# Attention and a bilinear feed-forward on one core: float64 weight words loaded two bytes off, their upper half made by a float16 conversion, raw words and gate outputs in planned slots

## The chip, the cores and the metric

The kernel runs on one core of one Trainium2 chip. The metric is the device time of one execution in microseconds; three executions give a median. A trace of one more execution shows every instruction of the five engines: TensorE (PE, with its weight loads as PEld), VectorE (DVE), ScalarE (ACT), GpSimd (POOL) and SyncE (SP, which here only issues DMAs).

## What is computed

Random-feature attention over 8 batches, 8 heads, 576 positions and head size 64, and then a feed-forward with a product of two projections in the middle. The four weights of the feed-forward are float64 arrays (a division of a float32 draw by a square root makes them so); the other inputs are float32.

```python
def phi(x):                                  # x scaled by D ** -0.25
    h = x @ omega.T - (x * x).sum(-1, keepdims=True) / 2
    return np.exp(h - h.max(-1, keepdims=True)) / np.sqrt(m)
q_p, k_p = phi(q_s), phi(k_s)                # 128 features
kv, z = k_p.T @ v, k_p.sum(2)                # per batch and head
x = (q_p @ kv) / (q_p @ z + 1e-6)            # to (4608, 512)
out = ((x @ w1) * (x @ w2) @ w3) @ w_out     # w1, w2: 512 x 1024; w3: 1024 x 1024; w_out: 1024 x 512
```

## The kernel before

**Stages.** The 4608 positions are 36 chunks of 128 rows. Each chunk of k and of q goes through `features`: a projection on omega into a bank pair of PSUM (`pa`), its row maximum (DVE), an exponential (ACT), and a split of the result into a float16 part and its float16 remainder. Products are then made of three float16 matmuls (`PASSES`). `kv_batch` sums keys with values, `q_attend` divides, `x_turn` scales a chunk and has it transposed by a DMA into `xT`. `gate` multiplies two chunks at a time by w1 and w2, multiplies both results, and splits the product into `h`; `project_out` multiplies `h` by W and writes the output. From chunk 28 to 33 `pair_first` and `pair_rest` do the last product with fewer multiplications, on mixed blocks of W made by `mix`.

**Weights.** W is the product of w3 and w_out, made on the chip in `W_block` in float32: eight blocks, four for the first half of the inner sum and four for the second, which `keep` adds up in `Wb`. w1 and w2 are split into float16 pairs in place, in `w12b`, after their absolute sums have given a scale. All weights come as raw 64-bit words, 20 loads of 1 MB (the first in two halves), and go through `from_float64`: `fetch` issues the load, `magnitude` takes on ACT the absolute value of the upper words read as float32, and `words` clamps it (on GpSimd, but for the first half), shifts it, merges in sign and exponent bits, and finally merges in the shifted lower word. The last three are passes of DVE over 1024 numbers in each of 128 partitions.

**Places.** Raw words, magnitudes and the gate's outputs live in one tile, `arena`, of 21 blocks of 2 KB a partition: three raw places of four blocks, two of magnitudes, five free. `block` hands places out, `used` takes them back, in the order in which the program is written; after the last weights the raw places go to the free list. Converted w_out and w3 are guests in `w12b[:, 1]`, the place of the second halves of w1 and w2; those can be loaded only after the products are done, and the second half of w_out after the first four blocks.

**Order.** Nothing runs as it is written. A planner (`Plan`) records every operation with its tiles and dependencies. `forward` plays the program with a cost for every operation, takes on each engine the ready one of least rank, gives tiles of a pool their slots, and `order` ranks again from the end backwards. Each engine then gets its own fixed order, SP too. Where the plan leaves TensorE idle for longer than 516 ns, `fill` puts matmuls of a tile of ones on themselves (`ones_bf`, 128x512) whose result nothing reads; they keep TensorE active. They are called fillers here. As one function fires all operations, all lines of the profile are L171; instructions are told apart by tile and shape.

**Softmax.** `DQ` and `DK` give for each chunk how the maximum is subtracted: "0" is a DVE subtraction from PSUM into `e` and one exponential of 1024 numbers, "1" is eight exponentials of 128 numbers straight from PSUM with the negated maximum as bias. `DQ` has "1" for three of the 36 chunks of q.

Of the kernel before, what the change touches and what calls it, by code (L numbers as in the profile page):

```python
# [12 lines left out]
U32 = mybir.dt.uint32  # L13
AF = mybir.ActivationFunctionType
# [12 lines left out]
F64_LEAST, F64_TOP = 2.0**-15, float.fromhex("0x1.dffffep+16")  # L27
# [7 lines left out]
CLAMP = "dp"  # L35
# [4 lines left out]
DQ = '100110000000000000000000000000000000000000'  # L40
# [52 lines left out]
ARENA = 21  # L93
# [155 lines left out]
class Plan:  # L249
# [112 lines left out]

    def forward(self, rank, deps, after, costs, slots=False, backwards=False, scale=0.0):

        start, end, waiting, ready = {}, {}, {}, {n: [] for n in LANES}
        clock = dict.fromkeys(LANES, 0.0)
        est = {}
# [28 lines left out]
        for _ in self.ops:  # L396
# [26 lines left out]
            clock[n] = t + busy  # L423
            if op.method.startswith("dma"):
# [38 lines left out]
    def order(self):  # L463

        ops = self.ops
        costs = {o: self.cost(o) for o in ops}

# [83 lines left out]
ROOM = {}  # L551
BANKS = ("pm", "pa")
# [5 lines left out]
WARM = True  # L558
HOP = 80
ROUNDS = 1  # L560
# [5 lines left out]
def tile_favor_attention_then_bilinear_ffn(  # L566
# [27 lines left out]
    DF = w1.shape[1] // 2  # L594
    NC = HD // P
    NF = DF // P
    DO = wo.shape[1] // 2
# [405 lines left out]

    arena = const.tile([P, ARENA, 512], F32, name="arena")
    raw_at = list(range(0, 4 * RAW64_BUFS, 4))
    mag_at = list(range(4 * RAW64_BUFS, 4 * RAW64_BUFS + 4, 2))
    free = list(range(4 * RAW64_BUFS + 4, ARENA))

    def block():
        assert free, "no block left"  # L1010
        return free.pop(0)

    left = {}
# [4 lines left out]
    def used(at):  # L1018

        left[at] -= 1  # L1020
        if not left[at]:
            free.append(at)

    def from_float64(new, src, name, cuts=1):
# [4 lines left out]
        def fetch():  # L1029
            at = st["at"] = raw_at.pop(0)  # L1030
            nfetch[0] += 1
            raw = arena[:, at : at + 4].bitcast(U32).rearrange("p b i -> p (b i)")

            raw = raw.rearrange("p (j i) -> p j i", j=src.shape[1])
            step = src.shape[1] // cuts
            for k in range(0, src.shape[1], step):
                {'a': nc.scalar, 's': nc.sync, 'p': nc.gpsimd}[pick(FQ, nfetch[0])].dma_start(raw[:, k : k + step], src[:, k : k + step])
            st["raw"] = raw.rearrange("p j i -> p (j i)").rearrange("p (i t) -> p i t", t=2)

        def magnitude():  # L1040

            at = st["mag"] = mag_at.pop(0)
            st["g"] = arena[:, at : at + 2].rearrange("p b i -> p (b i)")
            st["dst"] = new()
            for a in pieces:
                nc.scalar.activation(st["g"][:, a], st["raw"][:, a, 1].bitcast(F32), AF.Abs)

        def words():
            for a in pieces:
                g, dst = st["g"][:, a], st["dst"][:, a].bitcast(U32)  # L1050
                top, low = st["raw"][:, a, 1], st["raw"][:, a, 0]

                (nc.gpsimd if pick(CLAMP, nfetched.pop(0)) == "p" else nc.vector).tensor_scalar(
                    g, g, F64_TOP, F64_LEAST, ALU.min, ALU.max
                )
                g = g.bitcast(U32)
                nc.vector.tensor_scalar(
                    g, g, 3, 0x3FFFFFFF, ALU.logical_shift_left, ALU.bitwise_and
                )
                nc.vector.scalar_tensor_tensor(  # L1060
                    g, top, 0xC0000000, g, ALU.bitwise_and, ALU.bitwise_or
                )
                last = nc.vector.scalar_tensor_tensor(
                    dst, low, 29, g, ALU.logical_shift_right, ALU.bitwise_or
                )
            return last

        def bits():
            converted.append(words())
            raw_at.append(st["at"])  # L1070
            mag_at.append(st["mag"])
# [6 lines left out]
    def w12_load(n, i):  # L1078
# [4 lines left out]
        src = w[cc * P : (cc + 2) * P, 1024 * i : 1024 * (i + 1)].rearrange("(c p) f -> p c f", p=P)  # L1083
# [30 lines left out]
    guest = w12b[:, 1]  # L1114

    def wo_load(n):
        j = 2 * n
        at = j % HALF
        dst = guest[:, at : at + 2].rearrange("p j o -> p (j o)")
        src = wo[j * P : (j + 2) * P].rearrange("(j p) o -> p j o", p=P)  # L1120
        return from_float64(lambda: dst, src, f"wo_{j}", cuts=1 if n or not START else 2)
# [3 lines left out]
    def W_block(n):  # L1125

        i, j0 = n * 2 % NF, n * 2 // NF * HALF
        at = HALF + n % 2 * 2
        w3c = guest[:, at : at + 2].rearrange("p b i -> p (b i)")
        pss = []  # L1130

        def product():
            w = w3c.rearrange("p (j i) -> p j i", j=HALF)
            for k in range(2):
# [3 lines left out]
                for j in range(HALF):  # L1138
# [3 lines left out]
                        guest[:, j],  # L1142
# [15 lines left out]
        src = w3T[j0 * P : (j0 + HALF) * P, 2 * i * P : 2 * (i + 2) * P]  # L1158
        return from_float64(lambda: w3c, src.rearrange("(j p) i -> p j i", p=P), f"w3_{n}") + [
# [27 lines left out]
    hs = {}  # L1187

    def gate(c0, n, u):
# [20 lines left out]
        if LATE <= c0 < LATE_END:  # L1210
# [10 lines left out]
            places = [block() for _ in range(2)]  # L1221
            hi, lo = (
                arena[:, k].bitcast(F16)[:, 0 : 7 * P].rearrange("p (m s) -> p m s", s=P)
                for k in places
# [3 lines left out]
            hs[c0, u] = (hi, lo), places  # L1228
# [351 lines left out]
```

## Time and profile before

| | |
|---|---|
| median of three executions | 799.29 us (798.73 to 800.18) |
| the profiled execution | 798.87 us |
| its span, first to last instruction | 797.1 us |
| busy: PE / DVE / ACT / POOL | 783.7 / 610.9 / 452.6 / 262.5 us |
| mean granted clock of TensorE | 0.997 of full speed |
| DMA | 88.42 MB, mean 111 GB/s |

Busy time is counted as the union of an engine's instructions. A row of a group has busy time in us and then the mean of one instruction in ns; instructions overlap at their ends, so that the mean times the count is more than the busy time. A row of the timeline begins with its start and its length in us, and a bracket at its end says how long the engine stood idle before it and what released it.

### The profile page before, as it was taken

What the parts mean: (1) busy time and instruction counts of PE and PEld (TensorE: products, weight loads), DVE (VectorE), ACT (ScalarE), POOL (GpSimd) and SP (SyncE); (2) the same over time, 40 slices, a digit from 0 to 9 for tenths busy, and PEclk for the clock granted to TensorE, in tenths of its full rate; (3) what the DMA queues carried; (4) which work ended last, traced back from release to release, by engine and by line L of the source; (5) the groups of instructions that cost most, each with busy time, mean ns of one, the idle gap of its engine ahead of it and who ended that gap; (6) DMA issues with size and microseconds to landing.
All of it is one profiled execution on the core that took longest, in us unless ns stands there. A gap on an engine that the chain in (4) does not pass through costs nothing.

```text
span 797.1 us, 20482 instructions
## 1 busy us (share of the span) xinstructions
PE 783.7 (98%) x8591; PEld 596.0 (75%) x8591; DVE 610.9 (77%) x1136; ACT 452.6 (57%) x807; POOL 262.5 (33%) x228
## 2 busy tenths in 40 slices
PE   8999999999899999999999999999999999999998
PEld 4554657978687777868787778777777777789886
DVE  6799999967986698598768767698879985996411
ACT  6885759866573566567545655476555535433211
POOL 2122212124443244234452443333343332333110
PEclk9999999999999999999999999999999999999999
DMA  9877875354361445455354444245543332223101
GB/s 333 301 230 252 226 184 117 67 108 95 93 132 42 108 119 107 73 128 120 80 95 133 87 87 95 73 114 112 106 77 54 81 81 55 54 54 67 42 1 53
DMA packets 142620, 88.42 MB, mean 111 GB/s; under 512 B 116736, under 2 KB 117120, under 8 KB 142528
## 3 DMA queue, kind: packets, MB, share of 16 engines
q1 hardware_dynamic: 142016, 86.07, 44.8%
q8 instruction: 67, 1.10, 0.6%
q10 hardware_dynamic: 432, 0.79, 0.3%
q0 software_dynamic: 80, 0.26, 0.1%
q14 instruction: 25, 0.20, 0.1%
HBM read 49.35 MB, written 9.44 MB: 74 GB/s over the span
## 4 chain that ended last, share of the span: by engine, by line
PE 75%; DVE 14%; ACT 6%; issue 3%; DMA 1%; SPq 0%; POOL 0%; DVEq 0%; ACTq 0%
PE pm L171 63%; PE pa L171 12%; DVE arena L171 3%; DVE s_nm L171 2%; DVE w12b L171 2%; DVE e L171 1%; ACT arena L171 1%; DVE ek L171 1%; ACT junk L171 1%; DVE vhl L171 1%; DMA arena<-w3T 1%; ACT vhl L171 1%; ACT ek L171 1%; DVE hl L171 1%; ACT e L171 1%
## 5 line engine op out<-in xcount | busy, mean ns | idle before, releaser
L171 PE MATMUL pm<-xT,w12b 128*128 128x256 f16 (+1 forms) x3840 | 392.7, 262 | 0.3 <-DMA xT<-xhl 0.3
L171 PEld LDWEIGHTS <-w12b 128*128 128x128 f16 x3840 | 338.9, 98 | 39.3 <-DMA xT<-xhl 1.3
L171 PE MATMUL pm<-Wb,arena 128*128 128x512 f16 (+1 forms) x852 | 173.2, 360 | 0.0
L171 PEld LDWEIGHTS <-arena 128*128 128x128 f16 x996 | 95.8, 98 | 79.4 <-issue 0.3
L171 POOL TENSOR_TENSOR arena<-asb,arena 128x512 f16<-128x512 f32 x60 | 80.5, 1341 | 158.4 <-ACT arena L171 145.4
L171 DVE TENSOR_REDUCE s_nm<-pa 128x8 f32<-128x1024 f32 x72 | 87.3, 1215 | 41.7 <-PE pa L171 41.7
L171 ACT ACTIVATE e<-e,ln_e,s_es 128x1024 f32<-128x1024 f32 x55 | 67.8, 1238 | 73.9 <-DVE e L171 73.7
L171 POOL TENSOR_TENSOR eq<-e,eq 128x1024 f16<-128x1024 f32 x31 | 74.0, 2387 | 95.3 <-issue 41.7
L171 POOL TENSOR_TENSOR ek<-e,ek 128x1024 f16<-128x1024 f32 x26 | 57.1, 2196 | 93.2 <-ACT ek L171 88.0
L171 DVE TENSOR_TENSOR e<-pa,s_nm 128x1024 f32<-128x1024 f32 x59 | 71.6, 1217 | 2.1 <-DVE s_nm L171 0.5
L171 DVE TENSOR_TENSOR asb<-pm,asb 128x512 f32<-128x512 f32 x60 | 41.1, 686 | 36.5 <-PE pm L171 35.6
L171 ACT CAST arena<-asb 128x512 f16<-128x512 f32 x60 | 36.8, 613 | 39.5 <-DVE asb L171 39.5
L171 PE MATMUL pm<-w12b 128*128 128x512 f32 x128 | 56.7, 596 | 0.3 <-DVE s_ws L171 0.3
L171 POOL TENSOR_SCALAR arena<-arena 128x1024 f32<-128x1024 f32 (+1 forms) x20 | 22.6, 1131 | 97.4 <-ACT arena L171 97.4
L171 ACT ACTIVATE asb<-pm 128x512 f32<-128x512 f32 x60 | 35.2, 586 | 32.8 <-PE pm L171 30.4
L171 PE MATMUL pa<-om,hl 64*128 64x128 f16 x1320 | 46.6, 218 | 3.2 <-DVE hl L171 3.2
L171 PEld LDWEIGHTS <-hl 64*128 64x128 f16 x1320 | 37.4, 95 | 14.7 <-issue 9.5
L171 DVE SCALAR_TENSOR_TENSOR xhl<-xs,s_p2r,xhl 128x512 f16<-128x512 f32 x36 | 38.9, 1080 | 12.0 <-ACT xhl L171 12.0
L171 ACT ACTIVATE o<-pm,oscs 128x512 f32<-128x512 f32 (+1 forms) x31 | 20.8, 671 | 47.9 <-PE pm L171 47.8
L171 PEld LDWEIGHTS pm<-w12b 128*128 128x128 f32 x128 | 23.8, 190 | 27.7 <-issue 26.3
L171 PE MATMUL pa<-vhl,ek 128*128 128x65 f16 (+1 forms) x896 | 43.3, 205 | 0.0
L171 DVE SCALAR_TENSOR_TENSOR hl<-qraw,s_s,hl 128x512 f16<-128x512 f32 x30 | 33.7, 1125 | 9.1 <-ACT hl L171 9.0
(116 smaller groups left out, 977.0 us busy)
## 6 DMA issues: line engine op xcount, KB each, us to landing
vraw<-v SPq DMA_DIRECT2D x36, 256.0 KB, 2.9
qraw<-qT SPq DMA_DIRECT2D x35, 256.0 KB, 2.8
arena<-w3T SPq DMA_DIRECT2D x8, 1024.0 KB, 5.9
kraw<-kT SPq DMA_DIRECT2D x32, 256.0 KB, 3.1
arena<-w SPq DMA_DIRECT2D x8, 1024.0 KB, 6.7
out<-o SPq DMA_DIRECT2D x28, 256.0 KB, 2.5
arena<-wo SPq DMA_DIRECT2D x3, 1024.0 KB, 4.9
out<-e SPq DMA_DIRECT2D x6, 256.0 KB, 2.1
```

The costliest lines, as they stand in the source:

```text
L171: p.real = getattr(lanes[p.lane], p.method)(*args, **{k: real(a) for k, a in p.kwargs.items()})
```

## The change

The load of raw words is issued in 16-bit units into a slot of 2050 words, one unit behind its start. So every 64-bit word lies two bytes off, and two of its parts fall on boundaries of their own: its top 16 bits are a bfloat16 number, and the 32 bits under them (bits 16 to 47) an aligned word. A copy on ACT from bfloat16 to float16 turns the top into sign, five exponent bits and the mantissa bits, which, with the lowest exponent bits that the bfloat16 mantissa carried along, are the upper half of the float32. It is written to every second 16-bit place of one of two constant tiles, `top`, whose other halves are zero. One DVE pass shifts the aligned word right by 13 and merges it with `top`. Absolute value, clamp, shift and merge of the sign are gone.

The arena goes. Raw words and gate outputs share four slots of one pool ("big", 8200 bytes a partition), converted w3 and w_out and the mixing's sums four of another ("mag", 4096 bytes), and the planner hands them out. A group's gate outputs (two chunks) are one slot. The converted w_out and w3 are no longer guests in `w12b`. All chunks of q take the eight exponentials. The planner runs two rounds in place of one, and counts the port that DVE and GpSimd share: `locks` names the operations that hold it. A smaller scratch for GpSimd's DMAs makes room.

```diff
-DQ = '100110000000000000000000000000000000000000'
+DQ = '1'
-ARENA = 21
+BIGS = 4
+MAGS = 4
+TOPS = 2
...
+    @staticmethod
+    def locks(op):
+
+        if op.lane == "gpsimd":
+            return not op.method.startswith("dma")
+        if op.lane != "vector" or op.out.space == PSUM or op.method in ("tensor_reduce", "reciprocal"):
+            return False
+        wide = [a for a in op.ins if a.free_size() > 1]
+        if op.out.free_size() == 1 or any(a.space == PSUM for a in wide):
+            return False
+        return True
...
-            t = est[op]
+            t = max(est[op], port) if LOCK and op.locks else est[op]
...
+            if op.locks:
+                port = t + busy
...
-ROUNDS = 1
+ROUNDS = 2
...
-            raw = arena[:, at : at + 4].bitcast(U32).rearrange("p b i -> p (b i)")
+            raw = at.tile([P, 2050], F32, tag="big", name=f"raw_{name}", bufs=BIGS)
+            st["top"] = tops[nfetch[0] % TOPS]
+            rows = raw.bitcast(U16)[:, 1:4097].rearrange("p (j i) -> p j i", j=src.shape[1])
...
+            st["hi"] = raw.bitcast(BF16)[:, 4:4100].rearrange("p (i t) -> p i t", t=4)[:, :, 0]
+            st["mid"] = raw.bitcast(U32)[:, 1:2049].rearrange("p (i t) -> p i t", t=2)[:, :, 0]
...
-                nc.scalar.activation(st["g"][:, a], st["raw"][:, a, 1].bitcast(F32), AF.Abs)
+                copy(kind == "d", to[:, a], st["hi"][:, a])
...
-                    g, g, F64_TOP, F64_LEAST, ALU.min, ALU.max
-                    g, g, 3, 0x3FFFFFFF, ALU.logical_shift_left, ALU.bitwise_and
-                    g, top, 0xC0000000, g, ALU.bitwise_and, ALU.bitwise_or
-                    dst, low, 29, g, ALU.logical_shift_right, ALU.bitwise_or
+                    dst[:, a], st["mid"][:, a], 13, top[:, a], ALU.logical_shift_right, ALU.bitwise_or
...
-    guest = w12b[:, 1]
+            g = at.tile([P, 1024], F32, tag="mag", name=f"wo_{j}", bufs=MAGS)
...
-        place = block()
+            parts[c0] = at.tile([P, 2 * n, 512], F32, tag="big", name=f"h_{c0}", bufs=BIGS)
...
-    nc = bacc.Bacc("TRN2", target_bir_lowering=False, num_devices=1)
+    nc = bacc.Bacc("TRN2", target_bir_lowering=False, num_devices=1, dynamic_dma_scratch_size=2048)
```

How instructions stand on DVE near the start of the program, from the first halves of w_out on. Before (`arena` holds raw words and magnitudes, `w12b` takes the converted ones, `s_nm` is a row maximum):

```order
L171 TENSOR_SCALAR arena<-arena 128x512
L171 TENSOR_SCALAR s_nm_214<-s_nm_214 128x8
L171 TENSOR_SCALAR pm_81<-pm_81 128x1
L171 SCALAR_TENSOR_TENSOR arena<-arena 128x512
L171 TENSOR_SCALAR arena<-arena 128x512
L171 SCALAR_TENSOR_TENSOR w12b<-arena 128x512
```

After (`big` holds raw words, `top` the upper halves, `mag` takes the converted ones):

```order
L173 SCALAR_TENSOR_TENSOR mag_82<-big_78,top_74 128x512
L173 TENSOR_SCALAR s_nm_231<-s_nm_231 128x8
L173 SCALAR_TENSOR_TENSOR mag_82<-big_78,top_74 128x512
L173 TENSOR_SCALAR pm_84<-pm_84 128x1 x2
L173 RECIPROCAL s_s_40_85<-pm_84 128x1
L173 TENSOR_SCALAR unom<-pm_84 128x1
L173 SCALAR_TENSOR_TENSOR mag_264<-big_147,top_75 128x1024
```

Each converted piece is now one instruction, and the second w_out load's stands ahead of the next row maximum.

On SP, which issues the loads in order, around the second half of w_out. Before (`w` is w1 or w2, `w3T` is w3, `wo` is w_out):

```order
L171 DMA vraw_86<-v 128x512
L171 DMA vraw_167<-v 128x512
L171 DMA vraw_169<-v 128x512
L171 DMA vraw_180<-v 128x512
L171 DMA arena<-w 128x2x1024
L171 DMA_TRANSPOSE eqT_101<-eq_100 128x8x128
L171 DMA arena<-w3T 128x4x512
L171 DMA_TRANSPOSE eqT_101<-eq_100 128x8x128
L171 DMA arena<-w 128x2x1024
L171 DMA arena<-wo 128x2x1024 x2
L171 DMA arena<-w3T 128x4x512 x2
```

After:

```order
L173 DMA big_147<-w 128x2x2048
L173 DMA big_159<-wo 128x2x2048
L173 DMA kraw_124<-kT 128x512
L173 DMA_TRANSPOSE eqT_104<-eq_103 128x8x128
L173 DMA big_172<-wo 128x2x2048
L173 DMA_TRANSPOSE eqT_104<-eq_103 128x8x128
L173 DMA big_78<-w3T 128x4x1024
L173 DMA vraw_89<-v 128x512
L173 DMA vraw_174<-v 128x512
L173 DMA vraw_185<-v 128x512
L173 DMA vraw_229<-v 128x512
```

The two w_out loads now stand apart, ahead of the loads of v for the next batch, which stood ahead of them.

## Rows read from the trace of the kernel before

**Rows 1.** Three stretches: span, busy us and instructions by engine, clock, DMA, GB/s.

```profile
0.00:40.00 40.00, 37.26 (x234) 21.16 (x234) 27.32 (x52) 29.43 (x76) 8.60 (x18) 1.00 0.89 317
40.00:160.00 120.00, 117.42 (x1133) 80.48 (x1132) 116.93 (x200) 90.69 (x175) 25.06 (x37) 1.00 0.67 179
160.00:797.10 637.10, 629.00 (x7231) 494.35 (x7228) 466.68 (x886) 332.46 (x558) 228.88 (x175) 1.00 0.39 85
```

**Rows 2.** Groups by shape, busy us and mean ns: the fillers.

```profile
L171 PE MATMUL pm<-ones_bf 128*128 128x512 bf16 x123 | 29.7, 393 | 1.1 <-DVE sums L171 1.1
```

**Rows 3.** Timeline of PE: first fillers, first weight product, last fillers, last product.

```profile
1.12 3.53 PE L171 MATMUL pm<-ones_bf 128*128 128x512 bf16 x9 [1.12 <-DVE sums L171]
...
24.57 7.05 PE L171 MATMUL pm<-w12b 128*128 128x512 f32 x16
...
129.68 1.48 PE L171 MATMUL pm<-ones_bf 128*128 128x512 bf16 x6
...
783.00 10.58 PE L171 MATMUL pm<-Wb,arena 128*128 128x512 f16 x72
```

**Rows 4.** Timeline of all engines, 16 to 25 us: one w3 conversion.

```profile
16.40 1.15 ACT L171 ACTIVATE arena<-arena 128x1024 f32<-128x1024 f32 x1
...
17.64 1.26 POOL L171 TENSOR_SCALAR arena<-arena 128x1024 f32<-128x1024 f32 x1 [2.33 <-ACT arena L171]
...
23.23 1.21 DVE L171 SCALAR_TENSOR_TENSOR w12b<-arena 128x1024 uint32<-128x1024 uint32 x1
```

**Rows 5.** Groups by shape: conversion, a plain ACT cast, a DVE split pass.

```profile
L171 DVE SCALAR_TENSOR_TENSOR arena<-arena 128x1024 uint32<-128x1024 uint32 x19 | 24.8, 1306 | 0.2
...
L171 DVE SCALAR_TENSOR_TENSOR w12b<-arena 128x1024 uint32<-128x1024 uint32 x19 | 24.1, 1276 | 0.1
...
L171 ACT ACTIVATE arena<-arena 128x1024 f32<-128x1024 f32 x19 | 22.1, 1163 | 6.1 <-DVE w12b L171 3.8 <-DMA arena<-w3T 1.3 <-DMA arena<-w 1.0
L171 POOL TENSOR_SCALAR arena<-arena 128x1024 f32<-128x1024 f32 x19 | 22.0, 1158 | 89.1 <-ACT arena L171 89.1
...
L171 DVE TENSOR_SCALAR arena<-arena 128x1024 uint32<-128x1024 uint32 x19 | 13.9, 734 | 5.4 <-POOL arena L171 5.3
...
L171 DVE SCALAR_TENSOR_TENSOR w12b<-w12b,s_ws 128x512 f16<-128x512 f32 x16 | 12.1, 759 | 0.7 <-ACT w12b L171 0.6
...
L171 ACT CAST eq<-e 128x1024 f16<-128x1024 f32 x6 | 6.3, 1054 | 0.1
```

**Rows 6.** Groups by shape: the two ways to the exponential.

```profile
L171 DVE TENSOR_TENSOR e<-pa,s_nm 128x1024 f32<-128x1024 f32 x59 | 71.6, 1217 | 2.1 <-DVE s_nm L171 0.5
L171 ACT ACTIVATE e<-e,ln_e,s_es 128x1024 f32<-128x1024 f32 x55 | 67.8, 1238 | 73.9 <-DVE e L171 73.7
...
L171 ACT ACTIVATE e<-pa,s_nm 128x128 f32<-128x128 f32 x48 | 13.5, 390 | 0.0
...
L171 DVE TENSOR_SCALAR s_nm<-s_nm 128x8 f32<-128x8 f32 x13 | 4.8, 369 | 0.0
```

**Rows 7.** Timeline of SP's issues: the first w_out loads, the late ones.

```profile
2.01 1.53 SPq L171 DMA_DIRECT2D arena<-wo  x3
...
51.85 6.52 SPq L171 DMA_DIRECT2D arena<-wo  x2
```

**Rows 8.** DMA issues: count, KB each, median us to landing.

```profile
qraw<-qT SPq DMA_DIRECT2D x35, 256.0 KB, 2.8
...
arena<-w SPq DMA_DIRECT2D x8, 1024.0 KB, 6.7
...
eqT<-eq SPq DMA_TRANSPOSE x72, 3.2
```

**Rows 9.** Timeline of all engines near 206 us.

```profile
204.04 2.14 POOL L171 TENSOR_TENSOR ek<-e,ek 128x1024 f16<-128x1024 f32 x1 [0.63 <-DVE s_s L171]
204.08 4.20 DVE L171 SCALAR_TENSOR_TENSOR vhl<-vraw,s_s,vhl 128x512 f16<-128x512 f32 x2
...
209.06 1.25 PE L171 MATMUL pa<-om,hl 64*128 64x128 f16 x20 [2.79 <-DVE hl L171]
```

More of the change, by code (lines that the diff above doesn't have):

```diff
@@ L34 @@
 WS = "a"
-CLAMP = "dp"
+HS = "a"
 EH = 'daaaaadadaaadaaaaaaaaaaaaaaaa'
@@ L366, in forward @@
         clock = dict.fromkeys(LANES, 0.0)
+        port = 0.0
         est = {}
@@ L466, in order @@
         costs = {o: self.cost(o) for o in ops}
+        for o in ops:
+            o.locks = self.locks(o)
         def turned(deps):
@@ L1016, in tile_favor_attention_then_bilinear_ffn @@
     nfetched = list(range(99))
[L1018 to L1022, printed above, removed]
+    tops = []
+    for i in range(TOPS):
+        t = const.tile([P, 1024], F32, name=f"top_{i}")
+        nc.gpsimd.memset(t, 0.0)
+        tops.append(t)
     def from_float64(new, src, name, cuts=1):
@@ L1113, in tile_favor_attention_then_bilinear_ffn, with keep @@
     HALF = NF // 2
-    guest = w12b[:, 1]
+    guest = {}
     def wo_load(n):
         j = 2 * n
-        at = j % HALF
-        dst = guest[:, at : at + 2].rearrange("p j o -> p (j o)")
+        def keep():
+            g = at.tile([P, 1024], F32, tag="mag", name=f"wo_{j}", bufs=MAGS)
+            for k in range(2):
+                guest[(j + k) % HALF] = g[:, k * DO : (k + 1) * DO]
+            return g
         src = wo[j * P : (j + 2) * P].rearrange("(j p) o -> p j o", p=P)
-        return from_float64(lambda: dst, src, f"wo_{j}", cuts=1 if n or not START else 2)
+        return from_float64(keep, src, f"wo_{j}", cuts=1 if n or not START else 2)
     wam = const.tile([P, NF], F32, name="wam")
@@ L1220, in gate @@
             by.tensor_tensor(g[:, 7], g[:, 3], g[:, 6], ALU.subtract)
-            places = [block() for _ in range(2)]
+            if u % 2 == 0:
+                parts[c0, u // 2] = at.tile([P, 4, 512], F32, tag="big", name=f"h_{c0}_{u}", bufs=BIGS)
             hi, lo = (
-                arena[:, k].bitcast(F16)[:, 0 : 7 * P].rearrange("p (m s) -> p m s", s=P)
-                for k in places
+                parts[c0, u // 2][:, 2 * (u % 2) + k].bitcast(F16)[:, 0 : 7 * P].rearrange("p (m s) -> p m s", s=P)
+                for k in range(2)
             )
@@ L1274, in first @@
                 )
-            for _ in range(2):
-                at_.append(block())
-                left[at_[-1]] = 1
-                t.extend(arena[:, at_[-1], n * QN : (n + 1) * QN] for n in range(2))
+            m = at.tile([P, 4, QN], F32, tag="mag", name=f"mix_{j}", bufs=MAGS)
+            t.extend(m[:, n] for n in range(4))
             add(0, b12(0, j), (-1, b11(0, j)), (1, b12(1, j)), (-1, b11(1, j)))
@@ L1331, in pair_rest @@
         p34 = products(f"p34_{c0}", (c0, 6, b22), (c0, 1, n4))
-        for j in range(NJ):
-            for k in hs.pop((c0, j))[1]:
-                left[k] = 1
-                used(k)
         nc.vector.tensor_tensor(o[:, 1:3], o[:, 1:3], p34, ALU.add)
@@ L1360, in project_out @@
             queue.dma_start(out[c * P : (c + 1) * P, d], o[:, d])
-        for f in range(NF):
-            used(hs[c, f][1])
     LEAD = 5
@@ L1526, in tile_favor_attention_then_bilinear_ffn @@
         weights(n)
-        if not ticks and raw_at:
-            for a, w in [(a, 4) for a in raw_at] + [(a, 2) for a in mag_at]:
-                free.extend(range(a, a + w))
-            raw_at.clear()
         unit(RESERVE if t > EAGER else 0)
@@ L1575 @@
     with tile.TileContext(nc) as tc:
-        weights = [a.bitcast(U32) for a in args[4:]]
+        weights = [a.bitcast(U16) for a in args[4:]]
         tile_favor_attention_then_bilinear_ffn(tc, *args[:4], *weights, out)
```

83 lines of the change are left out of this document (32 added, 51 removed).

## The prediction

> **What bounds the kernel now.** I read the busy time by stage first [rows 1]. TensorE is busy 783.68 of 797.10 us, so nothing but TensorE's own time sets the end; every other engine has a quarter or more of the span free. But a busy TensorE is not yet useful work: the fillers, matmuls on `ones_bf` that the planner puts where it expects TensorE to wait, are 123 instructions and 29.7 us [rows 2]. So TensorE's work for the result is 783.7 - 29.7 = 754.0 us, and 43.1 us are filler or idle. The timeline of TensorE says where [rows 3]: the nine runs of fillers (9, 23, 21, 15, 12, 17, 5, 15 and 6) all lie before 132 us. In that stretch TensorE waits for weights: the first matmul that multiplies w3 by w_out begins at 24.57 us. After 160 us it is busy 629.00 of 637.10 us. Of the 13.4 us idle [rows 1], 1.12 are the start and 797.1 - 793.6 = 3.5 the last output's way out [rows 3]; 8.8 us are scattered. So there is something to win in the first 160 us only, and a change that lightens DVE, ACT or GpSimd later wins nothing.
>
> Why do the weights come late? From 40 to 160 us DVE is busy 116.93 of 120 us [rows 1]; that is the wait that ends last there. From 0 to 40 us the DMA engines are the fullest thing, 0.89 busy at 317 GB/s. One conversion on its way to the first product [rows 4] goes ACT (16.40), GpSimd (17.64), then three DVE passes between DVE's other work, the last at 23.23, and the matmul at 24.57 [rows 3]: 8.2 us.
>
> **The change part by part.** *Conversion.* Removed per megabyte of weights are the clamp, the shift and the merge of the sign; kept are one ACT pass and one last DVE pass. By the groups [rows 5], on DVE 0.734 + 1.306 us go each time, on GpSimd 1.158. There are 20 MB, so DVE loses 20 x 2.04 = 40.8 us, GpSimd some 23. The new ACT pass reads every fourth two-byte number and writes every second; no row has that. The nearest are the Abs that it replaces (stride two, 1.163) and a plain cast of 1024 (1.054): I take 1.16, so nothing changes on ACT. The new DVE pass is the old last one with other operands: 1.276. Nearly all of this work lies before 140 us, where DVE is the bound.
>
> *Softmax of q.* All 36 chunks now take their exponential straight out of PSUM, eight ACT instructions with a bias, where 33 took one DVE subtraction and one ACT exponential. Each loses 1.217 on DVE and gains a small one of 0.369, and on ACT 13.5/48 x 8 = 2.25 replaces 1.238 [rows 6]: DVE -28 us, ACT +33 us over the run. After 160 us both are hidden under TensorE (ACT 332 of 637 us). If that cover were gone, a chunk would cost about 1 us more on ACT. Up to the split of the combined weights the order of ACT has 7 such groups where it had 4, +3 us.
>
> *Slots.* Second-half weights of w_out no longer wait for their place in w12b, nor the second halves of w1 and w2 for the products to finish with it. Four raw slots stand where three stood; gate outputs share them, one slot for a group. SP's order shows it: the two late w_out loads stood in one block behind four v loads, and now stand apart and ahead of them. In the trace SP stood 6.52 us on that block [rows 7]. A load behind a full slot holds SP still, since SP issues in order; behind it wait q, k and the transposes.
>
> *Order.* The planner runs two rounds and counts the port that DVE and GpSimd share; every engine's order is new. What it gives I read from the instructions that exist: fillers fall from 123 to 65, 47 before the first product (68 before), 18 after it (55 before), none behind the second product. The first nine take 3.53 us as now; the other 56 at (29.70 - 3.53)/114 = 0.230 us make 12.9, together 16.4 us. **Fillers: -13.3 us.** That is the main term. It is cashed only if the weights come as early as the order has it; otherwise TensorE is idle in the filler's place.
>
> *Can the weights come that early?* Two checks. First product: it needs two w_out megabytes, one of w3 and the k chunks around them, some 4.2 MB, which at 317 GB/s are 13.3 us; with the 2.0 us until the first issue [rows 7] and one ACT and one DVE pass (2.4) it starts at about 17.7. TensorE's own rows ahead of it are 1.1 of start, 4.6 of work (four projections of k at about 1.15) and 3.53 + 38 x 0.230 = 12.3 of fillers, 18.0. That fits. First product of the second half: 13 weight megabytes (13.6 MB) and 16 tiles of 0.26 MB are ahead, 17.8 MB, 56.2 us at 317 GB/s, with the same 4.4 us 60.6. TensorE's rows ahead of it are 39.9 of work (those 4.6, four products at 7.05 [rows 3], 7.1 of projections and sums), 16.4 of fillers and 1.1, 57.4. So the DMA is 3.2 us late at the rate that it had; at 317/0.89 = 356 GB/s, all engines busy, it takes 54.4 and is not late. I take between, **+1.3 us**. Later products have more room: the third of the second half has 20.9 MB ahead of it, 70 us in this way, against 76 of TensorE (two more products and 4.4 of the rest).
>
> *Landing two bytes off.* No load in the trace lands off a word. The lower bound is nothing (the bytes are the same, and a move is not made smaller). The upper is the row of transposes, which move the same 256 KB in two-byte numbers and land in 3.2 us where plain loads of q take 2.8 [rows 8]: up to 1.14 times. That would add 43 x 0.14 = 6.0 us to the late product. I take nothing, since the rows of a weight load stay 2 or 4 KB whole, as in the loads that go.
>
> The Trainium skill (DMA: Bandwidth & Descriptors, "How a descriptor splits into AXI transactions") speaks against this part: a transfer that does not start on a 256-byte boundary costs an extra partial transaction. Stated for reads, it would by estimate make a 4 KB row 17 transactions for 16, 1.06 times, and the late product some 2.6 us later. No run here shows it so far.
>
> *The hole at 206 us.* TensorE waits 2.79 us for DVE, where two passes over 512 numbers, of a kind that takes 0.76 us elsewhere [rows 5], took 4.20 while GpSimd ran a pass of 2.14 beside them [rows 9]. A planner that counts the port should avoid some of it, or make another: **-1.4 us**, half; bounds 0 and -2.8.
>
> By the Trainium skill (SBUF — State Buffer, "SBUF: two separate sides") the port that DVE and GpSimd share is an exclusive lock held for a whole instruction. The 4.20 us agree; by that rule alone the whole 2.8 would go.
>
> Sum: 797.1 - 13.3 + 1.3 - 1.4 = 783.7 us of span. The profiled execution took 798.87, 1.8 more than its span, and lies 0.4 under the median: 785.9 us.
>
> **The rivals.** *The weights stay as late as they were.* The ACT pass and the landing of loads replace DVE as what ends last, and TensorE is idle where fillers stood. For: DMA is 0.89 busy to 40 us, and ACT would have to be 85% busy to 145 us with its 120.1 + 3 us, where it is now 120.1/160 = 75% [rows 1]. Against: DVE, fed in the same way, reached 97% for 120 us [rows 1]. If ACT cannot pass the 75%, its 123 us need 164 and all the gain is gone; half of it gives 791 to 798.
>
> *The idle goes with the fillers.* All 8.8 us scattered idle disappear too, since DVE has 69 us less to do: 797.1 - 13.3 - 8.8 + 1.8 + 0.4 = 777.2. For: the longest of them waits for DVE [rows 9]. Against: new orders make new holes.
>
> *Slower: the landing itself.* If a load that lands two bytes off takes f times as long, the first product of the second half is late by 3.2 + 43 x (f - 1), as every product before it is by a part of that. From f = 1 + (13.3 + 1.4 - 3.2)/43 = 1.27 the gain is gone; at f = 1.5 the span is 797.1 - 14.7 + 24.7 = 807, some 809 us; at 2 it would be 831. For: no row has such a landing. Against: even moves in two-byte numbers stand at 1.14.
>
> *The change doesn't do what it says.* The new ACT pass could be slow enough to undo the saving: at 2 us for 1.16, 20 x 0.84 = 17 us more on ACT before 110 us, where it then has nothing free. That is the first rival's time or a little more, 795 to 803.
>
> **How the numbers follow.** Forecast (780 to 791) 0.58; idle goes too (776 to 780) 0.10; weights stay late (791 to 797.7) 0.13; about where it is (797.7 to 800.9), from that and a slow ACT pass, 0.06; slower by the landing, or by a hole that the new order makes, 0.13. A measurement of this kernel can tell about 0.2%, 1.6 us, from no change. So faster 0.81, same 0.06, slower 0.13. The range from 776.5 to 800.0 leaves out the slower cases and a little below.
>
> **What would show it.** Right: the first product at 17 to 19 us; fillers of about 16 us; TensorE busy nearly whole from 30 us on; the GpSimd clamp and two DVE passes gone; DVE some 540 us, ACT some 485. Wrong: loads of w1 and w2 that take over 7.5 us to land where they took 6.7 [rows 8]; ACT's cast over 1.5 us; TensorE idle between 30 and 100 us naming ACT, DVE's last pass or a DMA; a busy time much over 770 us, which would be work at the lower clock after such idle.

## The result, and the profile after

The changed kernel takes 780.67 us, the median of four executions (778.22 to 781.41), against 799.24 us for the kernel before beside it: a ratio of 0.976, with an interval from 0.974 to 0.978. The forecast was 785.9; the time lies 5.2 us below it, inside the range. It is also inside the band of 780 to 791 us that the prediction held likeliest, but only by 0.7 us: the four executions stand on both sides of its edge. The profiled execution took 780.73, its span is 779.0.

I read the busy times first, as in [rows 1]. From the page of the kernel after, the line of busy times, and then the same three stretches as before (span, busy us and instructions by engine, clock, DMA share, GB/s):

```profile
PE 768.9 (99%) x8525; PEld 591.0 (76%) x8533; DVE 512.5 (66%) x1093; ACT 504.5 (65%) x1038; POOL 231.5 (30%) x210
```

```profile
0.00:40.00 40.00, 38.56 (x204) 19.88 (x209) 16.27 (x33) 29.35 (x74) 3.43 (x13) 1.00 0.94 346
40.00:160.00 120.00, 119.00 (x1266) 87.23 (x1268) 100.58 (x215) 104.65 (x222) 16.77 (x26) 1.00 0.73 182
160.00:779.00 619.00, 611.33 (x7062) 483.94 (x7060) 395.68 (x847) 370.49 (x744) 211.28 (x171) 1.00 0.38 85
```

TensorE is still what sets the end: idle 10.1 us, where it was 13.4. From 40 to 160 us DVE has come down from 116.93 to 100.58, ACT up from 90.69 to 104.65. The group of the fillers answers to [rows 2]:

```profile
L173 PE MATMUL pm<-ones_bf 128*128 128x512 bf16 x64 | 16.5, 414 | 1.1 <-DVE ones_bf L173 1.1
```

The program holds 65 of them; the trace lacks one record. The span is TensorE's work for the result, its fillers and its idle time. Before it was 754.0 + 29.7 + 13.4 us, after it is 752.4 + 16.5 + 10.1. So the 18.1 us that the span lost are 13.2 of fillers, 3.3 of idle and 1.6 of work. The same sum serves for every kernel below.

TensorE's timeline answers to [rows 3] (start, us, group):

```profile
1.09 4.02 PE L173 MATMUL pm<-ones_bf 128*128 128x512 bf16 x9 [1.09 <-DVE ones_bf L173]
...
7.96 8.43 PE L173 MATMUL pm<-ones_bf 128*128 128x512 bf16 x37
...
18.30 7.13 PE L173 MATMUL pm<-mag,mag 128*128 128x512 f32 x16
...
26.89 4.09 PE L173 MATMUL pm<-ones_bf 128*128 128x512 bf16 x18
...
55.39 5.47 PE L173 MATMUL pa<-vhl,ek 128*128 128x65 f32 x48
...
61.13 3.68 PE L173 MATMUL pa<-vhl,ek 128*128 128x65 f32 x32
64.64 3.67 PE L173 MATMUL pm<-mag,mag 128*128 128x512 f32 x8
```

The first product of w3 and w_out starts at 18.30 us where it started at 24.57, behind 46 of the 64 fillers; the other 18 stand behind it, and none after 31 us. The first product of the second half starts at 64.64 with no idle time before it, but only 0.08 us behind the last weight conversion ahead of it:

```profile
63.33 1.23 DVE L173 SCALAR_TENSOR_TENSOR mag<-big,top 128x1024 uint32<-128x1024 uint32 x1 [0.24 <-ACT top L173]
```

The new conversion against [rows 5], and the exponential against [rows 6] (groups by shape: busy us, mean ns):

```profile
L173 ACT ACTIVATE e<-pa,s_nm,s_es 128x128 f32<-128x128 f32 x240 | 87.4, 468 | 30.7 <-DVE s_nm L173 19.5 <-DVE s_gr L173 5.0 <-DVE s_mx L173 3.3
...
L173 ACT CAST top<-big 128x1024 f16<-128x1024 bf16 x19 | 25.9, 1379 | 4.9 <-DVE mag L173 2.7 <-DMA big<-w 2.2
...
L173 DVE SCALAR_TENSOR_TENSOR mag<-big,top 128x1024 uint32<-128x1024 uint32 x11 | 13.4, 1222 | 11.5 <-ACT top L173 11.5
```

ACT's new pass takes 1.379 us, not 1.16, and one chunk's eight exponentials 87.4/30 = 2.91, not 2.25. The hole of [rows 9] is not gone; it has moved. The stretch from 180 to 200 us, and of its timeline the passes that meet (a bracket is idle time and its releaser):

```profile
180.00:200.00 20.00, 16.67 (x159) 12.59 (x158) 18.81 (x41) 10.58 (x24) 8.25 (x5) 0.91 0.39 106
```

```profile
191.88 2.12 POOL L173 TENSOR_TENSOR eq<-e,eq 128x1024 f16<-128x1024 f32 x1 [0.68 <-POOL ek L173]
192.03 2.52 DVE L173 SCALAR_TENSOR_TENSOR hl<-qraw,s_s,hl 128x512 f16<-128x512 f32 x1 [0.28 <-ACT hl L173]
...
194.61 1.25 PE L173 MATMUL pa<-om,hl 64*128 64x128 f16 x20 [2.27 <-DVE hl L173]
```

The DVE pass started 0.15 us behind GpSimd's and ended 0.55 behind it, with 2.52 us for what takes 0.74 without such company (below). TensorE waited 2.27 us, and the granted clock of the stretch is 0.91.

### The profile page after: what moved, and what is told of

Read it like the earlier page. It is cut to its first block, busy times and chain, and to the rows that moved or that the text cites. A ratio compares the mean times of both kernels' runs of the same rounds, so it can differ in the third digit from the quotient of the medians.

```text
span 779.0 us, 20533 instructions
## 1 busy us (share of the span) xinstructions
PE 768.9 (99%) x8525; PEld 591.0 (76%) x8533; DVE 512.5 (66%) x1093; ACT 504.5 (65%) x1038; POOL 231.5 (30%) x210
## 4 chain that ended last, share of the span: by engine, by line
PE 87%; DVE 8%; ACT 3%; issue 1%; ACTq 0%; DVEq 0%
PE pm L173 73%; PE pa L173 14%; DVE mag L173 2%; ACT e L173 1%; DVE s_nm L173 1%; DVE Wb L173 1%; DVE w12b L173 1%; DVE vhl L173 1%; DVE hl L173 1%; ACT top L173 0%; ACT junk L173 0%; DVE ek L173 0%; DVE asb L173 0%; DVE xhl L173 0%; DVE xs L173 0%
## 5 line engine op out<-in xcount | busy, mean ns | idle before, releaser
L173 PE MATMUL pm<-Wb,big 128*128 128x512 f16 (+1 forms) x852 | 173.9, 361 | 0.0
L173 PEld LDWEIGHTS <-big 128*128 128x128 f16 x996 | 95.9, 98 | 80.2 <-issue 1.6
L173 POOL TENSOR_TENSOR big<-asb,big 128x512 f16<-128x512 f32 x60 | 78.0, 1299 | 160.5 <-ACT big L173 157.4
L173 ACT ACTIVATE e<-pa,s_nm,s_es 128x128 f32<-128x128 f32 x240 | 87.4, 468 | 30.7 <-DVE s_nm L173 19.5
L173 ACT CAST big<-asb 128x512 f16<-128x512 f32 x60 | 37.7, 628 | 44.9 <-DVE asb L173 44.8
L173 PE MATMUL pm<-mag,mag 128*128 128x512 f32 x128 | 57.4, 598 | 0.4 <-DVE mag L173 0.4
L173 PEld LDWEIGHTS pm<-mag,mag 128*128 128x128 f32 x128 | 23.6, 190 | 27.0 <-issue 25.6
L173 DVE CAST eq<-e 128x1024 f16<-128x1024 f32 x30 | 21.0, 699 | 29.7 <-ACT e L173 21.3
L173 ACT ACTIVATE e<-e,ln_e,s_es 128x1024 f32<-128x1024 f32 x25 | 31.5, 1258 | 13.4 <-DVE e L173 13.4
L173 POOL TENSOR_TENSOR big<-ek,big 128x896 f16<-128x896 f32 x12 | 22.8, 1897 | 41.2 <-ACT big L173 41.2
```

The lines of the kernel that those rows point to most:

```text
L173: p.real = getattr(lanes[p.lane], p.method)(*args, **{k: real(a) for k, a in p.kwargs.items()})
```

## The experiments

**Theories.** A, mine: the conversion is the main thing. Less work on DVE brings the weights earlier, so fillers go; planner, softmax and slots are worth a few us at most, and the place of the landing nothing. B: the planner's order is the main thing, and the fillers fell because it places work better. C: a load that lands two bytes off costs time, which something else covers. Each run names the kernel that it is an edit of. A row of the table is a median with its ratio to the kernel before run beside it, and from the trace the fillers, TensorE's idle time and its work.

| run | us | ratio | fillers us | idle us | work us |
|---|---|---|---|---|---|
| before | 799.2 to 800.3 | 1 | 29.7 | 13.4 | 754.0 |
| after | 780.67 | 0.976 | 16.5 | 10.1 | 752.4 |
| e1: after, old conversion | 791.28 | 0.989 | 27.6 | 9.9 | 751.0 |
| e2: before, new conversion | 782.34 | 0.978 | 17.3 | 10.9 | 752.6 |
| e3: after, aligned load | 780.24 | 0.976 | 16.5 | 9.3 | 751.5 |
| e4: after, old softmax | 777.76 | 0.972 | 16.5 | 9.1 | 750.6 |
| e5: after, old planner | 788.67 | 0.986 | 19.3 | 10.9 | 756.7 |
| e6: before, new planner | 792.37 | 0.991 | 32.9 | 8.8 | 749.4 |
| e7: before, no fillers | 807.9 | 1.010 | 0 | 33.4 | 773.3 |
| e8: after, cast on DVE | 781.17 | 0.976 | 17.9 | 9.1 | 752.6 |
| e9: before, new conversion and planner | 780.38 | 0.975 | 21.0 | 7.5 | 750.0 |
| e10: after, old softmax and planner | 786.91 | 0.983 | 18.4 | 13.4 | 753.5 |
| e11: after, planner blind to the port | 792.39 | 0.990 | 16.8 | 18.0 | 755.9 |
| e12: after, one pass from GpSimd to DVE | 778.70 | 0.973 | 17.1 | 7.8 | 751.1 |

**e1: the old conversion in the changed kernel.**

```diff
-                copy(kind == "d", to[:, a], st["hi"][:, a])
+                nc.scalar.activation(st["g"][:, a], st["raw"][:, a, 1].bitcast(F32), AF.Abs)
...
-                    dst[:, a], st["mid"][:, a], 13, top[:, a], ALU.logical_shift_right, ALU.bitwise_or
+                    g, g, F64_TOP, F64_LEAST, ALU.min, ALU.max
+                    g, g, 3, 0x3FFFFFFF, ALU.logical_shift_left, ALU.bitwise_and
+                    g, top, 0xC0000000, g, ALU.bitwise_and, ALU.bitwise_or
+                    dst, low, 29, g, ALU.logical_shift_right, ALU.bitwise_or
```

> The changed kernel with the old conversion put back (absolute value on ACT, clamp on GpSimd, three DVE passes, words loaded on a word boundary), in the new slots, with the new softmax and the new planner. Its program holds 114 fillers where the changed one holds 65. Theory: the two DVE passes and the clamp that each megabyte loses carry the gain, so 49 fillers come back, 49 x 0.23 = 11.3 us: about 792 us, from 789 to 796. Rival: the slots (four raw places, no guests in w12b) and the planner carry it; then it stays at 781 to 785.

Measured 791.28 us (790.3 to 791.9): 10.6 of the 18.6 us are lost. What stays, 8.8 us against the kernel before beside it, is about what the new planner gives alone (e6). The fillers are back:

```profile
L175 PE MATMUL pm<-ones_bf 128*128 128x512 bf16 x111 | 27.6, 398 | 1.2 <-DVE ln_e L175 1.1
```

**e2: the new conversion alone in the kernel before.**

```diff
-                nc.scalar.activation(st["g"][:, a], st["raw"][:, a, 1].bitcast(F32), AF.Abs)
+                nc.scalar.copy(to[:, a], st["hi"][:, a])
...
-                    g, g, F64_TOP, F64_LEAST, ALU.min, ALU.max
-                    g, g, 3, 0x3FFFFFFF, ALU.logical_shift_left, ALU.bitwise_and
-                    g, top, 0xC0000000, g, ALU.bitwise_and, ALU.bitwise_or
-                    dst, low, 29, g, ALU.logical_shift_right, ALU.bitwise_or
+                    dst, st["raw"][:, a, 0], 13, top[:, a], ALU.logical_shift_right, ALU.bitwise_or
```

> The kernel before with the new conversion alone: one ACT cast, one DVE pass; arena, guests, softmax and planner as before. The words are loaded on a word boundary, so the lowest mantissa bits of the weights are wrong; what is timed is the number and kind of passes. Its program holds 67 fillers. Theory: 799.2 - 56 x 0.23 = 786.3 us, from 783 to 790, with DVE some 40 us less busy. Rival (slots and planner carry the gain): 795 to 799.

Measured 782.34 us, 17.8 below the kernel before beside it, with 17.3 us of fillers. Theory A holds: with the old planner, old places and old softmax this one edit gives nearly all of the gain. DVE falls by 52.5 us to 558.4, more than the 40.8 removed. Of the passes that stay, the split of x (`xhl`) fell most, from 38.9 to 27.7 us for the same 36 passes; whether the clamp that GpSimd lost or the new order is behind it was not tried.

This kernel leaves out the right lower bits of the weights, and so do e3 and e9: on a word boundary the aligned 32 bits that the DVE pass merges are the lower word, and 19 of the 23 mantissa bits come from it, not only the lowest ones. The number, kind and shape of the passes are those of the new conversion.

**e3: the load on the word's start.**

```diff
-            rows = raw.bitcast(U16)[:, 1:4097].rearrange("p (j i) -> p j i", j=src.shape[1])
+            rows = raw.bitcast(U16)[:, 0:4096].rearrange("p (j i) -> p j i", j=src.shape[1])
...
-            st["hi"] = raw.bitcast(BF16)[:, 4:4100].rearrange("p (i t) -> p i t", t=4)[:, :, 0]
-            st["mid"] = raw.bitcast(U32)[:, 1:2049].rearrange("p (i t) -> p i t", t=2)[:, :, 0]
+            st["hi"] = raw.bitcast(BF16)[:, 0:4096].rearrange("p (i t) -> p i t", t=4)[:, :, 3]
+            st["mid"] = raw.bitcast(U32)[:, 0:2048].rearrange("p (i t) -> p i t", t=2)[:, :, 0]
```

> The changed kernel with the raw words loaded on a word boundary in place of two bytes off it; the DVE pass takes the lower words as they then stand, so the lowest mantissa bits are wrong. Everything else is the same, order included. Theory: landing off a boundary costs nothing that can be seen: 780.7 us, within 1.6, the loads of w1 and w2 landing in 6.9 us and those of w3 in 9.0. Rival: it costs, and the loads land earlier here; by one partial transaction in 16 the time would fall by up to 2.6 us.

Measured 780.24 us (779.1 to 780.9), 0.4 below the changed kernel, inside the spread of either. DMA issues with their median us to landing, of the changed kernel and then of e3:

```profile
big<-w3T SPq DMA_DIRECT2D x8, 1024.0 KB, 9.0
big<-w SPq DMA_DIRECT2D x8, 1024.0 KB, 6.9
```

```profile
big<-w3T SPq DMA_DIRECT2D x8, 1024.0 KB, 10.1
big<-w SPq DMA_DIRECT2D x8, 1024.0 KB, 6.5
```

One group lands later when aligned, the other sooner. w3 lands later in both than the 5.9 us of before, so the longer landing does not come from the two bytes. More was moved at that time: 359 GB/s from 20 to 40 us after the change and 370 in e3, where it was 301; that this is the reason was not tried. Theory C falls for this kernel. The Trainium skill's partial transaction (DMA: Bandwidth & Descriptors, "How a descriptor splits into AXI transactions") would have made an estimated 2.6 us; no such difference shows in these landings, which are writes into SBUF, while the section speaks of reads.

**e4: the old softmax.**

```diff
-DQ = '1'
+DQ = '100110000000000000000000000000000000000000'
```

> The changed kernel with the exponential of q as before (33 of 36 chunks with a DVE subtraction and one exponential of 1024 numbers). 66 fillers where the changed kernel has 65. Theory: the softmax moved 28 us off DVE and some 50 us onto ACT, both beside TensorE's work, so it is worth nothing: 780.9 us, within 2. Rival: DVE's lighter load took idle time out of TensorE, 3 us of it; then 783 to 786.

Measured 777.76 us (776.9 to 778.1), 2.9 below the changed kernel, where I expected no difference. It is the fastest version here, and beats both. ACT has 455.6 us instead of 504.5, DVE 537.2 instead of 512.5; neither ends last. But this order has no hole: TensorE is busy the whole stretch in which the changed kernel stalls.

```profile
180.00:200.00 20.00, 20.00 (x248) 15.45 (x247) 18.82 (x40) 10.21 (x18) 9.15 (x5) 1.00 0.54 122
```

Whether the exponentials or this one hole make the 2.9 us is what e12 was for.

**e5 and e6: the planner taken back, and the planner alone.** e5 is an edit of the kernel after; e6 puts `locks`, the port and the second round into the kernel before.

```diff
-LOCK = True
+LOCK = False
...
-ROUNDS = 2
+ROUNDS = 1
```

> The changed kernel with the planner as before: one round, the shared port not counted. 76 fillers for 65. Theory: the planner's part is small, 11 x 0.23 = 2.5 us: 783.2 us, from 781 to 786. Rival: counting the port spares holes in which DVE waits for GpSimd; then TensorE is idle in more places than now and it takes 786 to 792.

> The kernel before with the new planner alone (two rounds, the shared port counted); conversion, places and softmax as before. 133 fillers for 123. Theory: the planner finds nothing without the lighter conversion: 799.2 + 10 x 0.23 = 801.5 us, from 798 to 803. Rival: the port's holes (2.8 us at 206 us) go: 795 to 797.

Measured 788.67 and 792.37 us: the planner is worth 8.0 us in the changed kernel and 799.79 - 792.37 = 7.4 in the old one. By the table e5 loses 2.8 us of fillers, 0.8 of idle time and 4.3 of work. I had reckoned the planner by fillers, and in the old kernel they point the wrong way: e6 has 133 of them, more than before, and is still faster. It takes idle time, 13.4 to 8.8 us, and work, 754.0 to 749.4. Theory B is right in that the planner is not small; it does not take the fillers away, though. The fillers of e6, and its last stretch as in [rows 1]:

```profile
L171 PE MATMUL pm<-ones_bf 128*128 128x512 bf16 x133 | 32.9, 398 | 1.1 <-DVE sums L171 1.1
```

```profile
160.00:791.10 631.10, 627.01 (x7270) 496.04 (x7270) 441.02 (x887) 335.58 (x559) 222.11 (x175) 1.00 0.39 87
```

Behind 160 us TensorE is idle 4.1 us where it was 8.1, and in either 3.5 of them are the last output's way out. So 4.0 of the 4.6 us of idle time that the planner takes lie there.

**e7: the kernel before without fillers.** If fillers cost their time, this would show it.

```diff
-FIRST, GAP, UNTIL = 1500.0, 300.0, 200000.0
+FIRST, GAP, UNTIL = 1500.0, 300.0, 0.0
```

> The kernel before with all 123 fillers left out; they compute nothing that is used. Theory: a filler only marks a wait and costs nothing itself, so leaving them out does not bring their 29.7 us back: the time stays at 799 or rises, since TensorE then stands idle in the first 130 us and its granted clock falls after that; from 799 to 812. Rival: the fillers themselves push work back, and the gain of the change is that there are fewer: 770 to 790.

Measured 807.9 us, 8.1 more than the kernel before beside it. 29.7 us of fillers went, 20.0 of idle came, and work rose by 19.3. TensorE's timeline of e7 and its stretch from 40 to 160 us show why:

```profile
26.25 9.71 PE L171 MATMUL pm<-w12b 128*128 128x512 f32 x16 [4.51 <-DVE w12b L171]
```

```profile
40.00:160.00 120.00, 111.30 (x930) 77.67 (x932) 110.56 (x186) 87.46 (x171) 26.20 (x37) 0.91 0.68 183
```

The first product takes 9.71 us where it took 7.05 [rows 3], after 4.51 us idle. The trace's record of the granted clock begins only at 31.46 us, at full speed. If TensorE ran at the lower of the two levels, 1.2 GHz, until then, the product's first 5.21 us did the work of 2.6, and with the 4.50 that follow that makes 7.1 us, an estimate that fits. Behind it the record shows the lower level from 41.7 to 51.9 us and twice more before 160, so the granted clock of the stretch is 0.91.

So leaving the fillers out saves nothing here. Only 20.0 of their 29.7 us came back as idle time, though; how much of the other 9.7 the fillers cost by themselves this run cannot tell, since the lower clock makes the work longer at the same time. A filler marks a place where TensorE waits, and the time falls when the wait falls.

**e8: the cast on DVE.**

```diff
-HS = "a"
+HS = "d"
```

> The changed kernel with the cast of the upper 16 bits on DVE in place of ACT, all 20 MB. In the changed kernel ACT is the fuller engine from 20 to 60 us, DVE stands at a third to a half. 72 fillers for 65. Theory: the cast's place is not what ends last; the DVE then takes a second pass of 0.7 to 1.2 us per megabyte where it has room, and ACT loses 1.35: 779 to 784 us. Rival: ACT ends last in that stage, and it is faster, 774 to 778.

Measured 781.17 us (780.6 to 781.4), the same as the changed kernel. On DVE a cast takes 0.741 us instead of 1.379:

```profile
L173 DVE CAST top<-big 128x1024 f16<-128x1024 bf16 x19 | 14.1, 741 | 0.0
```

ACT loses 23 us and nothing ends sooner, so ACT's slow cast is not what the weights wait for.

**e9 and e10: which parts add up.** e9 is e2 with the planner of e6; e10 is the changed kernel with the edits of e4 and e5.

```diff
-DQ = '1'
+DQ = '100110000000000000000000000000000000000000'
...
-LOCK = True
+LOCK = False
...
-ROUNDS = 2
+ROUNDS = 1
```

> The kernel before with the new conversion (on a word boundary, lowest mantissa bits wrong) and the new planner; arena, guests and softmax as before. Against the changed kernel with the old softmax (777.8 us) it differs by the slots alone. 83 fillers where that one has 66. Theory: conversion alone gave 782.3 and the planner takes holes away later in the run; with the guests still in the way of the second-half loads the time is 776 to 781, so the slots are worth 0 to 3 us. Rival: the slots are worth what the fillers say, 17 x 0.23 = 3.9 us, or more: 781.7 us or above.

> The changed kernel with the old softmax and the old planner: new conversion and slots. 72 fillers. It stands between the conversion alone (782.3 us) and the changed kernel with the old planner (788.7 us). Theory: slots are worth little, and the new softmax's order made the holes that cost the latter: 781 to 785 us. Rival: the slots themselves cost under the old planner, by fewer places for gate outputs: 786 to 790.

Measured 780.38 and 786.91 us. e9 has the whole gain without the new slots and without the new softmax. The slots are worth 780.38 - 777.76 = 2.6 us with the new planner (e9 to e4) and cost 786.91 - 782.34 = 4.6 with the old one (e2 to e10); the first is small against the intervals, which meet at 0.9735. In e10, with the old softmax, TensorE is idle 3.26 us in the same stretch, in two gaps; the longer waits for DVE's subtraction of the maximum, so such holes are not the new softmax's alone:

```profile
180.00:200.00 20.00, 16.74 (x226) 14.36 (x224) 19.79 (x37) 10.90 (x18) 7.24 (x5) 1.00 0.51 131
```

```profile
191.38 0.89 PE L173 MATMUL pa<-kv,eqT 128*128 128x65 f16 x24 [2.14 <-DVE e L173]
```

So the parts are not a sum: 17.8 for the conversion and 7.4 for the planner give 19.9 together. Of the spans in the table 3.7 us are missing in e9 against e2 and e6 added up: 2.0 of work, 1.2 of idle time and 0.5 of fillers.

**e11: two rounds, blind to the port.**

```diff
-LOCK = True
+LOCK = False
```

> The changed kernel with two planner rounds, but the shared port of DVE and GpSimd not counted. 67 fillers. The old planner cost 8 us (788.7). Theory: the port is what the planner's new rule spares; without it DVE waits for GpSimd more, and TensorE for DVE: 785 to 790 us. Rival: the second round is what matters: 779 to 783.

Measured 792.39 us (791.0 to 793.4): counting the port is worth 11.7 us with two rounds; with one round it was not tried. A second round without it is 3.7 worse than one round (e5), hardly clear of noise, since the intervals of the two ratios still meet at 0.987. The instructions are the same, but DVE has 526.9 us of busy time instead of 512.5 and TensorE is idle 18.0 us. Near 165 us, GpSimd's rows and then DVE's (start, us):

```profile
160.72 2.43 POOL L173 TENSOR_TENSOR eq<-e,eq 128x1024 f16<-128x1024 f32 x1 [6.40 <-DVE s_p2r L173]
165.76 6.65 POOL L173 TENSOR_TENSOR big<-asb,big 128x512 f16<-128x512 f32 x1 [2.61 <-ACT big L173]
```

```profile
159.44 0.41 DVE L173 TENSOR_TENSOR mag<-mag,Wb 128x256 f32<-128x256 f32 x1
...
161.26 2.17 DVE L173 TENSOR_TENSOR mag<-mag,Wb 128x256 f32<-128x256 f32 x1
...
169.31 2.09 DVE L173 TENSOR_TENSOR mag<-mag,Wb 128x256 f32<-128x256 f32 x6
171.32 1.21 DVE L173 TENSOR_REDUCE s_nm<-pa 128x8 f32<-128x1024 f32 x1
...
174.29 0.18 DVE L173 TENSOR_SCALAR s_es<-pm,unom 128x3 f32<-128x3 f32 x1
```

Each engine holds up the other. A DVE pass that takes 0.41 us at 159.44, with GpSimd idle, takes 2.17 at 161.26 and ends 0.3 us behind GpSimd's; then a GpSimd pass of 1.3 us takes 6.65, to 172.41, beside a row of such DVE passes that has no gap until the row maximum at 171.32. DVE is busy all 20 us from 160 to 180. The small pass on `s_es` stands late in that queue, and TensorE waits for it. Two stretches of this run show a lowered clock, this one and another at 600 us:

```profile
174.53 2.29 PE L173 MATMUL pm<-xT,w12b 128*128 128x128 f16 x24 [2.88 <-DVE s_es L173]
```

```profile
160.00:180.00 20.00, 17.12 (x186) 12.01 (x184) 20.00 (x52) 8.65 (x13) 11.74 (x3) 0.91 0.37 93
600.00:620.00 20.00, 17.11 (x136) 13.03 (x137) 11.01 (x23) 8.85 (x18) 6.49 (x4) 0.83 0.41 79
```

```profile
602.89 8.15 PE L173 MATMUL pm<-xT,w12b 128*128 128x256 f16 x48 [3.33 <-DMA xT<-xhl]
```

At 600 us TensorE waits for a transposition by DMA, and the rows ahead of it show no meeting of such a length. So the port is shown for the gap at 174 us, and not for the whole 11.7.

The Trainium skill (SBUF — State Buffer, "SBUF: two separate sides") calls the shared port a lock held for a whole instruction, in which whoever starts first blocks the other. GpSimd's row at 160.72 and DVE's at 161.26 agree within 0.2 us, if the DVE pass of 0.41 runs behind GpSimd's; the 6.65 us fit, as a wait that goes on through a run of DVE passes.

**e12: the pass that makes the hole, moved.** The softmax stays new; one of GpSimd's passes, the one at 191.88, goes to DVE.

```diff
-QL = 'dddddppppppppppppppppppppp'
+QL = 'dddddppdppppppppppppppppppp'
```

> The changed kernel with one GpSimd pass of 2.1 us, the one beside which DVE's pass took 2.52 us at 192 us while TensorE waited 2.27, given to DVE (the remainder of chunk 7 of q). 67 fillers. Theory: the gap of 3.3 us in TensorE at 190 to 195 us and the 3.4 us at the lower clock behind it come from this meeting; without them 776.5 to 778.5 us, as with the old softmax, which had no such gap. Rival: the eight exponentials cost by themselves (2.9 us a chunk on ACT where 1.24 stood), and the gap comes back in another place: 780 to 782.

Measured 778.70 us (777.7 to 779.9), 2.0 less than the changed kernel; the intervals of the two ratios, up to 0.975 and from 0.974, overlap a little. The DVE pass that took 2.52 us takes 0.74, and the stretch has its full clock:

```profile
194.45 0.74 DVE L173 SCALAR_TENSOR_TENSOR hl<-qraw,s_s,hl 128x512 f16<-128x512 f32 x1
```

```profile
180.00:200.00 20.00, 18.44 (x196) 13.95 (x195) 18.75 (x45) 11.35 (x23) 6.58 (x4) 1.00 0.58 123
```

So some 2.0 of the 2.9 us of e4 go with this one hole, though the new plan moved other rows too. The 0.9 that is left between e12 and e4 is less than these runs can tell. The new softmax has no gain of its own that shows.

## Why the prediction was right, and where its sizes were not

**The main term: right.** The prediction put the gain into the first 160 us, through weights that come earlier, and let the fillers measure it. Fillers fell by 13.2 us where 13.3 stood, the first product began at 18.30 where 17 to 19 stood. e2 has nearly all of the gain with the conversion alone, and e1 loses 10.6 us of it without. e7 adds what was only taken for granted: the gain is not that fillers were left out, but that the wait under them went.

**"Something to win in the first 160 us only": wrong.** In the kernel before, 4.6 us of scattered idle time lay behind 160 us, 2.79 of them in the hole of [rows 9] and 1.27 in another wait for DVE:

```profile
365.76 0.90 PE L171 MATMUL pa<-kv,eqT 128*128 128x65 f16 x24 [1.27 <-DVE e L171]
```

e6 takes 4.0 of the 4.6 by order alone, and e4 and e12 win 2.9 and 2.0 us with orders that lack the hole at 192 us. The rival by which the idle time goes with the fillers, 777.2 us, got a chance of 0.10; the measured time is 3.5 us from it and 5.2 from the forecast, and e4 comes within 0.6.

**The weights of the second half: the step failed, and its term was 0, not +1.3.** Both sides of the comparison came later than reckoned. TensorE's rows ahead last until 64.64 us and not 57.4. The sums of keys and values are most of that: in this stretch they are float32 matmuls of 5.47 and 3.68 us, together more than the 7.1 us that I had for them and the projections beside them. The trace of before has them at the same lengths, and I had not read them there:

```profile
35.89 5.47 PE L171 MATMUL pa<-vhl,ek 128*128 128x65 f32 x48
...
55.41 3.68 PE L171 MATMUL pa<-vhl,ek 128*128 128x65 f32 x32
```

The last conversion ended at 64.56, where the two DMA reckonings gave 54.4 and 60.6. That the two misses met within 0.08 us may be the plan's doing or chance; whether the weights could have come sooner, had TensorE been ready, no run shows. In the rival "weights stay late", ACT's share of 75% was taken as a possible ceiling: ACT went to 104.65 of 120 us from 40 to 160, 87%, so it was none.

**The idle time: too little taken.** The sum left 12.0 us after the hole's half, and 1.3 for late weights. Measured are 10.1. From 0 to 160 us TensorE was idle 5.32 us before [rows 1] and is 2.44 after, and after 160 us 8.10 before and 7.67 after. So 2.9 of the 3.3 us came where the lighter DVE was thought to be worth only the fillers. With the 1.6 us less work and 0.5 of how the profiled execution stands to the median, this is the 5.2 us by which the forecast was high: 1.3 + 12.0 - 10.1 = 3.2, + 1.6, + 0.5, - 0.1 of fillers.

**The planner: mis-sized, and the sum near by luck.** I gave it 1.4 us for half of one hole. e5 and e6 give 8.0 and 7.4, e11 gives 11.7 for the port. The hole of [rows 9] itself was not halved but moved, from 206 to 192 us, 2.27 us where it was 2.79, and the idle time behind 160 us fell by 0.4. The forecast was still near because misses cancelled: conversion and planner take partly the same time (e9), and the new softmax, which I had at nothing, gave 2.9 back (e4). [rows 9] was also read too shortly. A second GpSimd pass stood right behind the one shown, so that two DVE passes took 4.20 us, more than 2.14 + 2 x 0.76 = 3.7:

```profile
206.13 1.60 POOL L171 TENSOR_TENSOR arena<-asb,arena 128x512 f16<-128x512 f32 x1
```

**ACT and DVE: the sizes were off.** "The ACT cast at 1.16" is 1.379: neither of the two neighbouring rows had a stride of four numbers. "2.25 a chunk" is 2.91, since the new exponential takes its scale as well as its bias from a column, 0.364 us each where [rows 6] had 0.281 with a bias alone. The Trainium skill (ScalarE: Activation LUTs, "What ACT_TABLE_LOAD costs") gives some 93 ns for each such operand; the rows here give 83. ACT ended at 504.5 us where "some 485" stood, DVE at 512.5 where "some 540" did; e11, with the port not counted, has 14.4 more on DVE. For the cast e8 shows that its size cost nothing. The softmax was not wholly hidden under TensorE, as the prediction had it: by e4 it cost 2.9 us, most of them by the one hole (e12).

**The landing: right.** Nothing was taken and nothing shows (e3), so the rival on the other side had no ground.

What stays open is the work: 754.0 us before, 749.4 to 756.7 in the other kernels with fillers, with the same matmuls (up to seven records of 8468 are missing in a trace). Part of it is time at the lower clock. With half of the busy time in those stretches taken off, it is 752.4 to 754.2 in the four kernels with one round and 749.4 to 751.4 in the nine with two. So some 2 us of the planner's worth are in the work itself; which rows became shorter, no run here takes apart.

## What to carry to other kernels

Where a wait is filled with work that nobody reads, price a change by how far the wait shrinks, and check it by taking the filler out: here that makes the kernel slower. Price an order by the passes that would meet on a shared port, row by row, and not by the number of fillers; the same instructions cost 780.7 or 792.4 us in two orders. And when a step moves earlier, price the work ahead of it by its own rows and type: float32 and float16 matmuls of one name stand in one kernel, and the trace of before shows which is where.

## What was not expected of the hardware

A copy on ACT that reads every fourth two-byte number and writes every second takes 1.379 us for 1024, against 1.054 for a plain cast [rows 5]; DVE does the same copy in 0.741. GpSimd can be held up as long as DVE: 6.65 us for a pass of 1.3, where in [rows 9] it was DVE that waited.
